# k^T v of batches 0 and 1 in full-width matmuls, and a part of expert 0's up projection around the last unit's values

## The chip, the cores and the metric

The kernel runs on one core of a Trainium2 chip (trn2). The metric is the device time of one execution in microseconds. Engines are named as in the profile: PE is TensorE's matmuls, PEld its weight loads, DVE is VectorE, ACT ScalarE, POOL GpSimd, SP SyncE, which here only issues DMAs.

## The reference

Linear attention with a decay per head (8 batches, 8 heads, 576 positions, head dimension 64), then a mixture of four experts over the 4608 x 512 result:

```python
scores = scale * q @ k^T                        # per batch and head, scale = 1/8
Dmat = where(rel >= 0, gamma[h] ** rel, 0)      # rel = position of q - position of k
x = ((scores * Dmat) @ v).transpose -> [4608, 512]
p = domain_probs / (domain_probs.sum(-1) + 1e-9)
out = sum over e of p[:, e] * (relu(x @ w1[e]) @ w2[e])     # w1: 4 x 512 x 1024, w2: 4 x 1024 x 512
```

## The kernel before

The decay is split into a factor on k and a factor on q, so that a chunk of positions needs three things: its own masked scores times v (`values_own`), its q times the sum of k^T v over all chunks before it (`values_carried`), and k^T v of its own for the chunks after it (`kv`). The 64 x 64 sums of two heads stand as diagonal blocks in a 128 x 128 tile of `sbd`, whose other blocks stay zero; so one matmul with 128 x 128 weights does a pair of heads.

Batches 0 and 1 are done in `Unit`s: four per batch, each half of 512 positions (`hf`) for four of the eight heads (`g`). Batch 0 comes first, in the order (hf, g) = (0,0), (1,0), (0,1), (1,1), called units 0 to 3 here; u is the index in the loop at L650. A unit's steps are:

- `cast` (L498): k and q times their decay to bf16 on DVE, v on POOL.
- `trans_pe` (L509): transposes of k and q on PE into `pt`, one ACT copy (L519) to `qkT`.
- `scores` (L531): 16 matmuls with 64 x 64 weights (L540), then the mask on DVE, `sT` (L542).
- `kv` (L547): matmuls into `kvp0` (L559), one per pair of rows r and half j of a head pair, with weights of 64 columns and 64 or 128 rows. The first block of a half sums 64 partitions, the second 128; in batch 0 a unit with hf = 1 also adds the whole first half. ACT copies both halves j to `sbd` (L578). In batch 1 the first half's total goes to `carry` with a DVE copy (L580), and the second half adds it while it writes `sbd` on DVE (L575).
- `values_own` (L586, L593), `values_carried` (L597, L603), then ACT copies the output to `xt` (L619), the transposed input of the experts: one call for each of two head pairs, which are two of the four 128-row parts (dc) of the up projection's contraction.

All PSUM tiles come from one ring of four buffers of two banks each (`ring_tile`). `warm(n)` (L135) issues n matmuls on zeros with 512 columns (L138).

The order on each engine is the program's order, written out by hand. After the loop of batch 0 the first tile of 512 tokens goes through the experts: `up_group` (L353) for pairs of 128-row parts of the hidden layer (i = 0 to 3; 16 matmuls of 512 columns at L359, relu on ACT at L363 for this tile), then `down_plain` (L372, L378) with its sums on DVE (L388, L390). Between these groups the steps of batch 1 and of batch 0's last 64 positions run at places given by the table `slots`: place n is run after group n. `v_head` is scores and kv of a unit of batch 1; units 2 and 3 of it have their transposes done by DMA from SP (L525). Weights are loaded on POOL's queue in a fixed order: w1 of expert 0 in two halves (`load_w1_at`), w2 of expert 0, w1 of expert 1 and so on. From the second tile on, the down projection uses seven products (L451) and the later batches use the class `Duo` with its own `kv` (L255), which the change leaves alone.

Of the kernel before, what the change touches and what calls it, by code (L numbers as in the profile page):

```python
# [11 lines left out]
Copy = mybir.ActivationFunctionType.Copy  # L12
Exp = mybir.ActivationFunctionType.Exp
Relu = mybir.ActivationFunctionType.Relu
# [9 lines left out]
def kernel(  # L24
# [10 lines left out]
    nc = tc.nc  # L35
    B, H, S, D = q.shape
# [9 lines left out]
    NDC = Dm // 128  # L46
# [19 lines left out]
    def ring_tile(name, shape, dt=FP32):  # L66
        return ring.tile(shape, dt, tag="ring", name=name)
# [25 lines left out]
    w1_sb = [const.tile([128, NDC, F], BF16, name=f"w1_{e}") for e in range(E)]  # L93
# [5 lines left out]
    def load_w1(e, f=slice(0, F)):  # L99
        return nc.gpsimd.dma_start(out=w1_sb[e][:, :, f], in_=moe_w1[e][:, f].rearrange("(dc p) f -> p dc f", p=128))  # L100
# [10 lines left out]
    NU = 4  # L111
# [23 lines left out]
    def warm(n):  # L135
        w = ring_tile("w", [128, 512])
        for _ in range(n):
            nc.tensor.matmul(w, lhsT=zz[:, 0:128], rhs=zz, start=True, stop=True)  # L138
# [69 lines left out]
    def mixing_weights():  # L208
        nc.vector.tensor_reduce(psm, prb, axis=mybir.AxisListType.X, op=ADD)
        nc.vector.tensor_scalar_add(psm, psm, 1e-9)  # L210
        nc.vector.reciprocal(psm, psm)
        nc.vector.tensor_tensor(pn, prb[:, :, :].rearrange("p t e -> p e t"),
                                psm.unsqueeze(1).to_broadcast([128, E, NTT]), op=MULT)
        nc.sync.dma_start(out=pd[:, :].rearrange("e (p t) -> p e t", p=128), in_=pn)
# [3 lines left out]
    def load_p(t, e, eng):  # L218
        pB[t, e] = ppool.tile([128, NT], FP32, tag="pB", name="pB")
        eng.dma_start(out=pB[t, e], in_=pd[e:e + 1, t * NT:(t + 1) * NT].to_broadcast([128, NT]))  # L220
# [4 lines left out]
    def xt_of(t):  # L225
        if t not in xt:
            xt[t] = xpool.tile([128, NDC, NT], BF16, tag="xt", name="xt")
        return xt[t]


    class Duo:
        def __init__(self, b, d):
            self.b, self.d = b, d
            self.ps = slice(2 * d, 2 * d + 2)
            self.qT, self.kT, self.sT = {}, {}, {}
# [14 lines left out]
        def kv(self):  # L250
            kvp = ring_tile("kvp", [128, 2, NC, D])
            for i, p in self.pairs():
                for c in range(NC):
                    for j in range(2):
                        nc.tensor.matmul(kvp[64 * j:64 * j + 64, i, c:NC, :], lhsT=bfs[p % 2]["k"][:, c, j, :],  # L255
                                         rhs=bv[p][:, c, j, :].unsqueeze(1).to_broadcast([128, NC - c, D]),
                                         start=(i == 0 and c == 0), stop=(c == NC - 1), skip_group_check=True)
            for j in range(2):
                r = slice(64 * j, 64 * j + 64)
                nc.scalar.activation(sbd[r, self.ps, :, r], kvp[r], Copy)  # L260
# [92 lines left out]
    def up_group(h, t, e, i):  # L353
        ph = ring_tile("ph", [128, 2, NT])
        x = xt_of(t)
        for f in range(2):
            fc = 2 * i + f
            for dc in range(NDC):
                nc.tensor.matmul(ph[:, f, :], lhsT=w1_sb[e][:, dc, fc * 128:(fc + 1) * 128],  # L359
                                 rhs=x[:, dc, :], start=(dc == 0), stop=(dc == NDC - 1))  # L360
        fk = e * NFC + 2 * i
        if t == 0:
            nc.scalar.activation(h[:, fk:fk + 2, :], ph, Relu)  # L363
            return
        nc.vector.scalar_tensor_tensor(h[:, fk:fk + 2, :], ph, 0.0,  # L365
                                       pB[t, e][:, :].unsqueeze(1).to_broadcast([128, 2, NT]), op0=MAX, op1=MULT)
        if i == NFC // 2 - 1 and t + 1 < n_nt:
            load_p(t + 1, e, nc.gpsimd)

    acc0 = {}  # L370

    def down_plain(h, t, e, ns):  # L372
        m, g = divmod(ns, 2)
        if g == 0:
            acc0["po"] = ring_tile("po", [128, 2, Dm])
        po = acc0["po"]
        for fc in range(NFC):
            nc.tensor.matmul(po[:, g, :], lhsT=h[:, e * NFC + fc, ns * 128:(ns + 1) * 128],  # L378
                             rhs=wx[e // 2][:, (e % 2) * NFC + fc, :, :].rearrange("p a b -> p (a b)"),
                             start=(fc == 0), stop=(fc == NFC - 1))  # L380
        if g == 0:
            return
        if e == 0:
            acc0[m] = spool.tile([128, 2, Dm], FP32, tag="S", name="acc0")
        for g in range(2):
            pe = pm0[:, 2 * m + g, e:e + 1]
            if e == 0:
                nc.vector.tensor_scalar_mul(acc0[m][:, g, :], po[:, g, :], pe)  # L388
            else:
                nc.vector.scalar_tensor_tensor(acc0[m][:, g, :], po[:, g, :], pe, acc0[m][:, g, :], op0=MULT, op1=ADD)  # L390
        if e == E - 1:
            for g in range(2):
                n0 = t * NT + (2 * m + g) * 128
                nc.sync.dma_start(out=out[n0:n0 + 128, :], in_=acc0[m][:, g, :])
# [95 lines left out]
    class Unit:  # L490
# [54 lines left out]
                tri0[:, :, :, :].rearrange("p r s t -> p (r s t)").unsqueeze(1).to_broadcast([128, 4, 2 * C]), op=MULT)  # L545

        def kv(self):  # L547
            kvp = ring_tile("kvp0", [128, 2, 2, D])
            hf = self.hf

            def mm(g, rows, dst, hh, first):
                for r in range(2):
                    for j in range(2):
                        lhsT = self.bf("k", hh)[0:rows, r, 2 * g + j, :]
                        rhs = self.bf("v", hh)[0:rows, r, 2 * g + j, :]
                        o = kvp[64 * j:64 * j + 64, g, dst, :]
                        if dst == slice(0, 2):
                            rhs = rhs.unsqueeze(1).to_broadcast([rows, 2, D])
                        nc.tensor.matmul(o, lhsT=lhsT, rhs=rhs, start=(first and r == 0), stop=False,  # L559
                                         skip_group_check=True)  # L560

            first = True
            for g in range(2):
                if hf == 1 and self.carry is None:
                    mm(g, 128, slice(0, 2), 0, first)
                    first = False
                mm(g, 64, 0, hf, first)
                first = False
                mm(g, 128, 1, hf, False)
            gs = slice(2 * self.g, 2 * self.g + 2)  # L570
            for j in range(2):
                jr = slice(64 * j, 64 * j + 64)
                dst = sbd[jr, gs, 2 * hf:2 * hf + 2, jr]
                if hf == 1 and self.carry is not None:
                    nc.vector.tensor_tensor(dst, kvp[jr],  # L575
                                            self.carry[jr, gs, :].unsqueeze(2).to_broadcast([64, 2, 2, D]), op=ADD)
                else:
                    nc.scalar.activation(dst, kvp[jr], Copy)  # L578
            if hf == 0 and self.carry is not None:
                nc.vector.tensor_copy(self.carry[:, gs, :], kvp[:, :, 1, :])  # L580

        def values(self):
            self.values_own()
# [53 lines left out]
    def cast_unit(u):  # L637
        us[u].cast("k", nc.vector)
        us[u].cast("q", nc.vector)
        us[u].cast("v", nc.gpsimd)  # L640
        if u in load_w1_at:
            load_w1(*load_w1_at[u])
# [7 lines left out]
    for u in range(NU):  # L650
        if u + 2 < NU:
            cast_unit(u + 2)
        us[u].values_own()
        if u + 1 < NU:
            us[u + 1].scores()
        us[u].values_carried()
        if u + 2 < NU:
            us[u + 2].trans_pe(1)
        if u + 1 < NU:
            us[u + 1].kv()  # L660
        if u == NU - 2:
            warm(2)
    mixing_weights()
    early.close()
    hp = ctx.enter_context(tc.tile_pool(name="hp", bufs=1))
    h = hp.tile([128, E * NFC, NT], BF16, name="h")
    first = ctx.enter_context(ExitStack())
    fpool = first.enter_context(tc.tile_pool(name="fpool", bufs=1))
    q1 = fpool.tile([128, 2, 2, 4, D], BF16, name="q1")
# [43 lines left out]
    def run(slots, i):  # L713
        for f in slots.get(i, []):
            f()
# [33 lines left out]
    n = 0  # L749
    for e in range(E):  # L750
        for i in range(4):
            up_group(h, 0, e, i)
            run(slots, n)
            n += 1
        for m in range(4):
            down_plain(h, 0, e, m)
            run(slots, n)
            n += 1
# [13 lines left out]
    for b in range(2, B):  # L772
        g = NS * (b - 3)
# [24 lines left out]
    for t in range(1, n_nt):  # L798
        d = [Down(h, t, s) for s in range(2)]
# [5 lines left out]
        n = NS * (t - 1)  # L805
# [40 lines left out]
```

## Time and profile before

| what | value |
|---|---|
| median of 4 runs | 536.35 us (535.85 to 536.38) |
| profiled execution | 536.37 us, span 534.7 us |
| PE busy | 527.5 us, 99% of the span |
| DVE, POOL, ACT busy | 361.6, 146.3, 87.2 us |
| chain that ended last | PE 95%, DVE 2%, ACT 1%, DMA 1% |
| granted TensorE clock | nine tenths or more of full speed in every slice of the page |
| DMA | 63.56 MB, 119 GB/s over the span |

Times in the views are microseconds from the start of the span. A busy PE is a PE with a matmul in flight, so its share says little by itself; the chain says what a later end hangs on. In the groups and timelines a line gives start, busy time, engine, line, operation, output<-inputs, the shape and count, and in brackets the idle time before it with what ended it.

### The profile page before, as it was taken

Reading aid. Unit: us, or ns where it says so; the run is one execution under the profiler, and the core shown is the slowest. Engines: PE = TensorE matmul, PEld = TensorE weight load, DVE = VectorE, ACT = ScalarE, POOL = GpSimd, SP = SyncE. Lnnn points to the kernel's source line nnn. Section 1 sums busy time; section 2 is a strip of 40 time slices with the busy share of each in tenths; the row PEclk is TensorE's granted clock in tenths of the full one; section 3 lists DMA queues with packets and bytes.
Section 4 is the critical chain, followed back from the end, with each engine's and each line's share of the span. In section 5 each row is a group of like instructions: output and inputs, shape, how many; then the busy total and the mean of one; then the engine's idle time right before and its main releaser. Section 6 shows DMA issues by size and latency. Waiting matters only on the chain.

```text
span 534.7 us, 10343 instructions
## 1 busy us (share of the span) xinstructions
PE 527.5 (99%) x4318; PEld 339.5 (63%) x4318; DVE 361.6 (68%) x454; ACT 87.2 (16%) x175; POOL 146.3 (27%) x188
## 2 busy tenths in 40 slices
PE   8999999999999999999999999999999999999997
PEld 4544454468745885478646865587548844884586
DVE  6425668896587767797578767777765567556754
ACT  4623450012101121020101001100110000000010
POOL 5734004245235344335132603153000000000000
PEclk9999999999999999999999999999999999999999
DMA  9999947678768766726353744454010111110001
GB/s 243 207 209 250 237 122 190 148 170 155 153 153 170 160 148 150 174 67 161 104 137 97 150 133 113 106 119 125 21 41 24 56 40 39 40 44 18 0 31 50
DMA packets 145119, 63.56 MB, mean 119 GB/s; under 512 B 124240, under 2 KB 135888, under 8 KB 145072
## 3 DMA queue, kind: packets, MB, share of 16 engines
q1 hardware_dynamic: 134752, 43.50, 34.5%
q0 software_dynamic: 10176, 19.27, 16.2%
q8 instruction: 34, 0.56, 0.4%
q10 hardware_dynamic: 144, 0.13, 0.1%
q14 instruction: 13, 0.11, 0.1%
HBM read 53.56 MB, written 9.51 MB: 118 GB/s over the span
## 4 chain that ended last, share of the span: by engine, by line
PE 95%; DVE 2%; ACT 1%; DMA 1%; issue 0%; SPq 0%; DVEq 0%
PE ph L359 47%; PE pd L451 37%; PE po L378 5%; PE kvp L255 1%; PE o L280 1%; PE s L269 1%; PE o L284 1%; ACT qkT L519 1%; DMA raw_0q<-in_q_dram 1%; DVE h L365 0%; DVE sT L542 0%; PE kvp L559 0%; PE s L540 0%; PE pt L517 0%; PE o L603 0%; PE w L138 0%
## 5 line engine op out<-in xcount | busy, mean ns | idle before, releaser
L359 PE MATMUL ph<-xt,w 128*128 128x512 bf16 x1152 | 254.7, 379 | 0.4 <-DVE h L365 0.2
L365 DVE SCALAR_TENSOR_TENSOR h<-ph,pB 128x1024 bf16<-128x1024 f32 x128 | 156.5, 1224 | 57.7 <-PE ph L359 57.7
L359 PEld LDWEIGHTS <-w 128*128 128x128 bf16 x1152 | 110.9, 98 | 129.5 <-issue 0.6
L451 PEld LDWEIGHTS <-h 128*128 128x128 bf16 x1024 | 99.8, 98 | 13.2
L451 PEld LDWEIGHTS <-s 128*128 128x128 bf16 x768 | 75.0, 98 | 8.7
L451 PE MATMUL pd<-wx,h 128*128 128x256 bf16 x512 | 61.1, 273 | 0.0
L451 PE MATMUL pd<-wx,s 128*128 128x256 bf16 x512 | 61.1, 273 | 0.0
L220 POOL DMA_DIRECT2D pB<-pd x28 | 15.7, 562 | 155.6 <-DVE h L365 142.7
L486 POOL TENSOR_TENSOR ob<-v,p 128x256 f32<-128x256 f32 x15 | 11.7, 783 | 114.3 <-DVE v L483 92.8
L239 POOL TENSOR_TENSOR bf_k<-raw_k,gk 128x512 bf16<-128x512 f32 x24 | 25.9, 1079 | 31.6 <-DMA raw_k<-in_k_dram 20.0
L260 ACT ACTIVATE sbd<-kvp 64x512 bf16<-64x512 f32 x24 | 14.2, 592 | 121.5 <-PE kvp L255 121.3
L271 DVE TENSOR_TENSOR sT<-s,tri 128x1024 bf16<-128x1024 f32 x24 | 28.3, 1219 | 7.5 <-PE s L269 7.5
L428 DVE TENSOR_TENSOR s<-s,h 128x1024 bf16<-128x1024 bf16 x32 | 30.9, 1006 | 0.0
L451 PE MATMUL pd<-t4w,h 128*128 128x256 bf16 x256 | 30.6, 273 | 0.0
L451 PE MATMUL pd<-t2w,s 128*128 128x256 bf16 x256 | 30.6, 273 | 0.0
L451 PE MATMUL pd<-t3w,h 128*128 128x256 bf16 x256 | 30.6, 273 | 0.0
L378 PE MATMUL po<-wx,h 128*128 128x512 bf16 x128 | 29.1, 379 | 0.1
L459 ACT ACTIVATE p<-pd 128x256 f32<-128x256 f32 x16 | 6.2, 384 | 138.9 <-PE pd L451 106.2
L239 POOL TENSOR_TENSOR bf_q<-raw_q,gq 128x512 bf16<-128x512 f32 x24 | 27.2, 1134 | 3.4 <-DMA raw_q<-in_q_dram 2.8
L432 DVE TENSOR_TENSOR s<-h,s 128x1024 bf16<-128x1024 bf16 x32 | 25.6, 839 | 0.0
L426 DVE TENSOR_TENSOR s<-h 128x1024 bf16<-128x1024 bf16 x32 | 23.8, 784 | 0.0
L468 DVE TENSOR_TENSOR u<-pd,p 128x256 f32<-128x256 f32 x16 | 6.8, 425 | 23.9 <-PE pd L451 23.8
(153 smaller groups left out, 364.6 us busy)
## 6 DMA issues: line engine op xcount, KB each, us to landing
pB<-pd POOLq DMA_DIRECT2D x28, 256.0 KB, 3.6
raw_k<-in_k_dram SPq DMA_DIRECT2D x48, 128.0 KB, 2.5
raw_q<-in_q_dram SPq DMA_DIRECT2D x48, 128.0 KB, 2.9
raw_v<-in_v_dram SPq DMA_DIRECT2D x48, 128.0 KB, 3.0
wx<-in_moe_w_dram POOLq DMA_DIRECT2D x4, 1024.0 KB, 15.3
out_dram<-oa SPq DMA_DIRECT2D x16, 256.0 KB, 2.2
out_dram<-ob SPq DMA_DIRECT2D x15, 256.0 KB, 2.4
w<-in_moe_w_dram POOLq DMA_DIRECT2D x3, 1024.0 KB, 15.1
```

The source lines that it names most:

```text
L220: eng.dma_start(out=pB[t, e], in_=pd[e:e + 1, t * NT:(t + 1) * NT].to_broadcast([128, NT]))
L239: eng.tensor_tensor(bfs[p % 2][n], raw1[n], g[:, :, 2 * p:2 * p + 2].unsqueeze(3).to_broadcast([128, NC, 2, D]), op=MULT)
L260: nc.scalar.activation(sbd[r, self.ps, :, r], kvp[r], Copy)
L271: nc.vector.tensor_tensor(sT[:, :, :, :].rearrange("p j c t -> p (j c) t"), s[:, :, :, :].rearrange("p j c t -> p (j c) t"), tri[:, :].uns ...
L359: nc.tensor.matmul(ph[:, f, :], lhsT=w1_sb[e][:, dc, fc * 128:(fc + 1) * 128], rhs=x[:, dc, :], start=(dc == 0), stop=(dc == NDC - 1))
L365: nc.vector.scalar_tensor_tensor(h[:, fk:fk + 2, :], ph, 0.0, pB[t, e][:, :].unsqueeze(1).to_broadcast([128, 2, NT]), op0=MAX, op1=MULT)
L378: nc.tensor.matmul(po[:, g, :], lhsT=h[:, e * NFC + fc, ns * 128:(ns + 1) * 128], rhs=wx[e // 2][:, (e % 2) * NFC + fc, :, :].rearrange("p ...
L426: nc.vector.tensor_tensor(self.alloc("s1")[:, l], h[:, l, self.b], h[:, r, self.b], op=ADD)
L428: nc.vector.tensor_tensor(self.alloc("s2")[:, l], self.s1[:, l], h[:, l, self.a], op=SUB)
L432: nc.vector.tensor_tensor(self.alloc("s4")[:, l], h[:, r, self.a], self.s2[:, l], op=SUB)
L451: mm = nc.tensor.matmul(dst, lhsT=src[:, kk, tok], rhs=rhs(c), start=(start and c == 0), stop=(c == KH - 1), skip_group_check=True)
L486: nc.gpsimd.tensor_tensor(self.ob[:, HF:Dm], self.v, self.p5, op=ADD)
```

## The change

In `kv` both heads of a pair are taken together: weights of 128 columns and a right side of 128 columns (256 where the first half is added for two blocks) give 128 x 128 products, of which only the diagonal blocks are read. `kvp0` grows to a full bank, the 128-row matmuls of both pairs g come first and the 64-row ones last. The copies to `sbd` read the diagonal blocks; the copy to `carry` is made per half j.

The first two of the four up groups of expert 0 (tile 0) are cut by tokens instead: `UpHalf(0)` is hidden parts 0 to 3 for tokens 0 to 255, `UpHalf(1)` the same for tokens 256 to 511. Eight of the 16 matmuls of `UpHalf(0)` are issued before the values of batch 0's last unit, the other eight right after them, and `UpHalf(1)` follows. `warm(2)`, which stood between unit 3's kv and its values, is gone.

```diff
+    class UpHalf:
+        def __init__(self, half):
+            self.c = slice(256 * half, 256 * half + 256)
+            self.ph = ring_tile("ph", [128, 4, 256])
+
+        def matmuls(self, i):
+            for fc in range(2 * i, 2 * i + 2):
+                for dc in range(NDC):
+                    nc.tensor.matmul(self.ph[:, fc, :], lhsT=w1_sb[0][:, dc, fc * 128:(fc + 1) * 128],
+                                     rhs=xt_of(0)[:, dc, self.c], start=(dc == 0), stop=(dc == NDC - 1))
+
+        def relu(self, h):
+            nc.scalar.activation(h[:, 0:4, self.c], self.ph, Relu)
...
         def kv(self):
-            kvp = ring_tile("kvp0", [128, 2, 2, D])
+            kvp = ring_tile("kvp0", [128, 2, 2, 128])
             hf = self.hf
-
-            def mm(g, rows, dst, hh, first):
+            first = [True]
+
+            def mm(g, rows, dst, hh):
                 for r in range(2):
-                    for j in range(2):
-                        lhsT = self.bf("k", hh)[0:rows, r, 2 * g + j, :]
-                        rhs = self.bf("v", hh)[0:rows, r, 2 * g + j, :]
-                        o = kvp[64 * j:64 * j + 64, g, dst, :]
-                        if dst == slice(0, 2):
-                            rhs = rhs.unsqueeze(1).to_broadcast([rows, 2, D])
-                        nc.tensor.matmul(o, lhsT=lhsT, rhs=rhs, start=(first and r == 0), stop=False,
-                                         skip_group_check=True)
-
-            first = True
+                    two = lambda n: self.bf(n, hh)[0:rows, r, 2 * g:2 * g + 2, :].rearrange("p j d -> p (j d)")
+                    rhs = two("v")
+                    if dst == slice(0, 2):
+                        rhs = rhs.unsqueeze(1).to_broadcast([rows, 2, 128])
+                    nc.tensor.matmul(kvp[:, g, dst, :], lhsT=two("k"), rhs=rhs, start=first[0], stop=False,
+                                     skip_group_check=True)
+                    first[0] = False
+
+            if hf == 1 and self.carry is None:
+                for g in range(2):
+                    mm(g, 128, slice(0, 2), 0)
             for g in range(2):
-                if hf == 1 and self.carry is None:
-                    mm(g, 128, slice(0, 2), 0, first)
-                    first = False
-                mm(g, 64, 0, hf, first)
-                first = False
-                mm(g, 128, 1, hf, False)
+                mm(g, 128, 1, hf)
+            for g in range(2):
+                mm(g, 64, 0, hf)
             gs = slice(2 * self.g, 2 * self.g + 2)
             for j in range(2):
                 jr = slice(64 * j, 64 * j + 64)
                 dst = sbd[jr, gs, 2 * hf:2 * hf + 2, jr]
+                src = kvp[jr, :, :, jr]
                 if hf == 1 and self.carry is not None:
-                    nc.vector.tensor_tensor(dst, kvp[jr],
+                    nc.vector.tensor_tensor(dst, src,
                                             self.carry[jr, gs, :].unsqueeze(2).to_broadcast([64, 2, 2, D]), op=ADD)
                 else:
-                    nc.scalar.activation(dst, kvp[jr], Copy)
-            if hf == 0 and self.carry is not None:
-                nc.vector.tensor_copy(self.carry[:, gs, :], kvp[:, :, 1, :])
+                    nc.scalar.activation(dst, src, Copy)
+                if hf == 0 and self.carry is not None:
+                    nc.vector.tensor_copy(self.carry[jr, gs, :], kvp[jr, :, 1, jr])
...
     for u in range(NU):
         if u + 2 < NU:
             cast_unit(u + 2)
+        if u == NU - 1:
+            part = UpHalf(0)
+            part.matmuls(0)
         us[u].values_own()
...
         if u + 1 < NU:
             us[u + 1].kv()
-        if u == NU - 2:
-            warm(2)
+    part.matmuls(1)
     mixing_weights()
     early.close()
     hp = ctx.enter_context(tc.tile_pool(name="hp", bufs=1))
     h = hp.tile([128, E * NFC, NT], BF16, name="h")
+    part.relu(h)
+    part = UpHalf(1)
+    part.matmuls(0)
+    part.matmuls(1)
+    part.relu(h)
...
     for e in range(E):
         for i in range(4):
-            up_group(h, 0, e, i)
+            if e > 0 or i > 1:
+                up_group(h, 0, e, i)
             run(slots, n)
```

## The prediction, made before the changed kernel had run

> **What bounds the kernel now.** The profiled execution took 536.37 us, its span is 534.7; the median of the four runs is 536.35. Sums are made on the span and taken off the median one for one. First the page: busy shares and chain.
>
> ```profile
> PE 527.5 (99%) x4318; PEld 339.5 (63%) x4318; DVE 361.6 (68%) x454; ACT 87.2 (16%) x175; POOL 146.3 (27%) x188
> ...
> PE 95%; DVE 2%; ACT 1%; DMA 1%; issue 0%; SPq 0%; DVEq 0%
> ```
>
> TensorE carries 95% of the chain, so only less work on PE, or less waiting by it, can count. Next the chain in order of time, where the change sits (start, length, what):
>
> ```profile
> 17.52 1.07 PE kvp L559 x24
> 18.59 0.54 PE w L138 x2
> ...
> 19.84 0.47 ACT xt L619
> ...
> 20.35 6.72 PE ph L359 x30
> ```
>
> Before 20.35 the chain passes between ACT and PE; from there PE is nearly alone. Then PE's timeline of that place (start, busy us, line, out<-in, weights, output, count, idle before):
>
> ```profile
> 16.41 0.41 PE L540 MATMUL s<-qkT 64*64 64x128 bf16 x13
> 17.05 0.25 PE L540 MATMUL s<-qkT 64*64 64x128 bf16 x3 [0.23 <-issue]
> 17.23 0.29 PE L603 MATMUL o<-qkT,sbd 128*128 128x128 bf16 x2
> 17.45 1.14 PE L559 MATMUL kvp<-bf_v,bf_k 128*64 128x128 bf16 x24
> 18.52 0.61 PE L138 MATMUL w<-zz 128*128 128x512 bf16 x2
> 19.05 0.42 PE L593 MATMUL o<-sT,bf_v 64*64 64x128 bf16 x16
> 19.40 0.40 PE L603 MATMUL o<-qkT,sbd 128*128 128x128 bf16 x4
> 19.64 1.09 PE L359 MATMUL ph<-xt,w 128*128 128x512 bf16 x3
> ```
>
> Two matmuls of zeros (L138) stand between kv and values. The first up projection starts at 19.64, does two matmuls, and stops: by single starts the third is at 20.346 and the fourth at 20.651, each 50 ns after one of the two ACT copies of xt (from 19.84) ends. The seventeenth, the first of group i=2, which the change leaves as it is, starts at 23.458. That is the point I compare.
>
> **Rates**, start to start of single matmuls in this trace: the same shape of weights in a row 56 ns for 128 columns, 109 for 256 (24.45 us for 224 at L451), 216 for 512. Where the shape of the weights changes (128x128, 128x64, 64x64), the next matmul starts about 93 ns after the stream ends: 149 after 128 columns (L593 to L603), 122 to 128 after 64, 309 after 512 (L138 to L593). In kv the two halves j start 3 ns apart, so they already run side by side.
>
> **kv of batch 0.** From the matmul before it to the one after it, kv takes 872, 1215, 870 and 1218 ns for units 0 to 3, with up to five changes of shape. The wide form for units 1 and 3: 56 (the matmul before has 128x128 weights as well), four of 256 columns 428, four of 128 columns 168 to the last, change 149, three steps of 67, 56, 56, change 149: 1129, which is 0.09 us less. Units 0 and 2: 701, 0.17 less. Of this unit 0 gives nothing, since ACT starts its sbd copy when qkT is done, and unit 2 nothing for the same reason. Unit 1 gives 0.09: its sbd copy at 13.41 waits for kvp, and ACT would be free at 13.32; all later links follow. The 64-row step with 128x128-wide output is a form that this trace lacks; between no change of shape at all and a change at every step, I take one change in and one out, as between 128x64 and 64x64 here.
>
> That the halves j run side by side (3 ns) speaks against going wide, but the changes of shape fill most of the old 1.07 us. The Trainium skill, TensorEngine Tiling (Array Packing), Theoretical Speedup, says that a stationary side of up to 64 columns, packed twice, runs up to twice as fast; by that alone, as an estimate, wide kv would double in units 1 and 3 and in batch 1, and the sum would end some 2 us slower than before.
>
> **The pause.** At 16.6 to 17.05 PE stands still within scores, and the view names no releaser ("issue"). It comes after some 448 matmuls and weight loads; the new order has 56 fewer by then and reaches that count only within values of unit 3, some 2.5 us later. I take it as gone. Then the two L603 of unit 2 wait for the sbd copy instead, which by the 0.09 above ends at 16.92: they start at 16.97 instead of 17.23, of which 0.17 is due to the pause.
>
> **Around the last values.** From there: second L603 at 17.04, kv from 17.10, its next at 18.17. Eight matmuls of 256 columns (108 each) take the place of the zeros; the last starts at 18.93, values at 19.13 (107 + 93), L603 at 19.48 to 19.65, eight more from 19.71, the half for tokens 256 to 511 from 20.57. Its third and fourth need the xt copies: ACT starts 0.256 after the last L603, at 19.91, and by the old lengths these are through at 20.42 and 20.73; PE wants them at 20.79 and 20.90. So no wait is left. Sixteen of 108 end at 22.30, where i=2 starts: 1.16 less than 23.458. The extra 16 weight loads are hidden (98 ns under 108), and two relu calls of 1024 elements replace two, in the same places of ACT's queue; no DMA moves in its queue. Covers: the first half of w1 lands at 17.15 (issue 9.35, 7.8 to landing), wanted at 18.17; the first w2 at 25.19 by its landings, wanted at 25.7 instead of 26.9; xt of unit 2 at 18.12, wanted at 18.49; and q of batch 1's first unit, landed at 49.79, is cast at 51.16, then 50.1. Past these covers each wait would give back its own length.
>
> **Batch 1.** In the middle kv follows scores, both with 64x64 weights:
>
> ```profile
> 66.92 0.77 PE L559 MATMUL kvp<-bf_v,bf_k 64*64 64x64 bf16 x16
> ...
> 68.53 0.29 DVE L580 COPY carry<-kvp 128x128 f32<-128x128 f32 x1 [0.17 <-ACT sbd L578]
> ...
> 82.51 0.17 PEld L603 LDWEIGHTS <-sbd 128*128 128x128 bf16 x3 [0.32 <-DVE sbd L575]
> ```
>
> Here the old form needs no change at its start: 748 ns. The new: 149 + 67 + 56 + 56 + 149 + 179 + 149 = 805. So 0.06 is lost in each of units 0 and 1; in units 2 and 3 it goes into PE's waits for DVE (0.19 at 81.75 and the line above). The carry copy becomes two, and the order of the new kernel shows that ACT's second sbd copy waits for DVE's first carry copy, which stands behind sT (68.4). ACT's second copy ends near 69.13 instead of 68.50, DVE's second carry copy at 69.47 instead of 68.82, and behind it the four casts of units 2 and 3 with their DMA transposes on SP, 0.7 later. q of unit 2 landed at 73.40, wanted at 75.19: hidden. The pB and raw loads behind them on SP are 0.7 later too; the first raw remainder is then cast near 87.4 and needed after 94. L603 of unit 1 wants sbd at 69.80, relu of i=1 moves by 0.15 and PE needs its buffer at 73.4.
>
> Sum: -1.16 + 0.11 = -1.05 us, so 535.3. From 20 to 84 us PE otherwise waits only for relu (0.2 four times), which moves along.
>
> **Rivals.** A, as summed, 535.0 to 535.5: chance 0.58. C, going from 128 to 64 rows at full width is no change of shape: two changes less (0.19) in unit 3 and 0.13 below the old time in each of batch 1's units 0 and 1, so -1.16 - 0.19 - 0.26 = -1.6, 534.7: 0.19. For it speaks that the output columns stay 128 wide; against it, every change of rows in kv costs 122 or more. The same page of the skill, Key Properties, says that a change of tiling mode drains TensorE, and lists 64x128 as a mode of its own; that would leave A. D, the pause comes back at its old count, which is then within values of unit 3, on a PE without slack: -1.16 + 0.50 + 0.11 = -0.55, 535.8: 0.08. B, slower: weights of 64 rows and 128 columns are never loaded ahead, so each of the three steps in a kv costs a whole change. At 149 that is 0.28 per kv: +0.26 in unit 1, +0.28 in unit 3, +0.56 in two of batch 1, +0.13 in the others beyond DVE's cover: +0.18 in all, 536.5. At 268, the longest step after a kv (79.47 to 79.74), it is 0.64 per kv and some +2.3, 538.7. It turns slower at about 140 per step. Chance 0.15.
>
> **Numbers.** 0.2%, about what a measurement of this kernel can tell from no change, is 1.07 us, 535.28, in the middle of A. A gives faster 0.34 and same 0.24; C faster 0.19; D same 0.08; B slower 0.12 and same 0.03. The range takes in C, D and the lower end of B: 534.6 to 536.5.
>
> **What would show it.** Right: no idle PE from the first kv of unit 3 to group i=2, which starts near 22.3; wide kv at 56 per step with two changes; the two carry copies 0.7 apart with scores of unit 2 unmoved behind ph. Wrong: steps of 150 between 64-row matmuls (B), none above 67 (C), a gap without releaser in values of unit 3 (D), or a wait for w1, w2 or xt where I count a cover.

## The result, and the profile after

The changed kernel takes 535.52 us (median of 38 runs, 534.85 to 537.8), the kernel before beside it 536.36 (60 runs). The ratio is 0.9984 with a 95% interval of 0.9979 to 0.9989: 0.86 us less, between 0.6 and 1.1. The interval leaves out no change, so it is faster, but by less than the 0.2% (1.07 us) that the prediction called no change. The forecast was 535.3.

Two points on counting. An up group is eight matmuls of 512 columns (L359 has 32 for the four groups of expert 0), not 16 as the description of the kernel before has it; the two groups that were cut are 16 of 512, or 32 of 256 columns. And some records of matmuls are missing from some traces, so that a count such as x15 in a view below can stand for 16.

The profiled execution of the changed kernel took 536.1 us, with a span of 534.4, against 536.37 and 534.7. So this one trace shows only 0.3 of the 0.86 us, and the question is what the other executions had that this one lacked. The page first, the busy shares and the chain:

```profile
PE 527.1 (99%) x4260; PEld 340.3 (64%) x4260; DVE 360.1 (67%) x456; ACT 87.2 (16%) x175; POOL 145.0 (27%) x188
...
PE 93%; DMA 3%; SPq 2%; DVE 1%; issue 0%; POOL 0%; DVEq 0%
```

PE's busy time hardly moved. The line to look at is the chain: DMA holds 3% instead of 1%. The chain in order of time, from 12 to 30 us (start, length, what), says which transfers these are:

```profile
9.57 5.24 DMA raw_3v<-in_v_dram
...
14.86 0.55 POOL bf_v L520
15.41 10.97 DMA wx<-in_moe_w_dram
26.38 0.14 issue
26.52 3.61 PE po L394 x16
```

In the kernel before, this stretch of the chain was PE's and ACT's. Now it is read backwards so: the first down projection (`po`, L394) starts 0.14 after w2 of expert 0 landed, at 26.38; w2 was issued at 15.41, because its issue stands on POOL's queue behind the cast of v of unit 3; and that cast waited for its own load until 14.81. So here PE waits for a load that the prediction had landed at 25.19, before it was wanted. PE's own line says the same (from the timeline of 25 to 27.5 us):

```profile
26.52 1.24 PE L394 MATMUL po<-wx,h 128*128 128x512 bf16 x5 [0.29 <-DMA wx<-in_moe_w_dram]
```

PE's timeline of the changed place (start, busy us, line, out<-in, weights, output, count, idle before):

```profile
16.57 0.42 PE L556 MATMUL s<-qkT 64*64 64x128 bf16 x16 [0.25 <-ACT qkT L535]
17.23 0.28 PE L619 MATMUL o<-qkT,sbd 128*128 128x128 bf16 x2 [0.24 <-ACT sbd L594]
17.35 1.15 PE L574 MATMUL kvp<-bf_v,bf_k 128*128 128x256 bf16 x12
18.43 1.05 PE L380 MATMUL ph<-xt,w 128*128 128x256 bf16 x8
19.41 0.42 PE L609 MATMUL o<-sT,bf_v 64*64 64x128 bf16 x16
19.76 0.40 PE L619 MATMUL o<-qkT,sbd 128*128 128x128 bf16 x4
19.99 2.78 PE L380 MATMUL ph<-xt,w 128*128 128x256 bf16 x24
22.61 0.59 PE L359 MATMUL ph<-xt,w 128*128 128x512 bf16 x2
```

From 17.35 to the group i=2 (L359 at 22.61) no line has an idle time in brackets: the zeros are gone, the 24 matmuls run through, and the wait for xt is gone with them. The scores before it run as 16 in one group, without the pause. In batch 1, from the timeline of all engines between 60 and 78 us:

```profile
66.69 0.72 PE L574 MATMUL kvp<-bf_v,bf_k 128*128 128x128 bf16 x8
...
67.95 0.27 DVE L596 COPY carry<-kvp 64x128 f32<-64x128 f32 x1
68.25 0.38 ACT L594 ACTIVATE sbd<-kvp 64x256 bf16<-64x256 f32 x1 [0.43 <-DVE carry L596]
68.67 0.29 DVE L596 COPY carry<-kvp 64x128 f32<-64x128 f32 x1 [0.45 <-ACT sbd L594]
```

The two carry copies start 0.72 apart, as the order of instructions had said; in the order of time the next thing on DVE, the casts, starts at 68.99 instead of 68.74, which is 0.58 later counted from the scores of unit 1 (66.34 here, 66.67 before), where the prediction had 0.7. No wait of PE grows by it: batch 1 loses 0.115 in all, and the two kv ahead of the casts account for that below.

To set runs side by side whose first loads came at other times, the experiments use distances between starts of single matmuls: t0 is the start of the last transpose of unit 3, i=2 the first matmul of the third up group, `po` the first matmul of the first down projection, and after it come the first transposes of batch 1, the first matmul of the second tile of tokens (tile 1), and the last matmul.

| distance, us | before | after | after, without its wait |
|---|---|---|---|
| t0 | 15.019 | 15.183 | |
| t0 to i=2 | 8.435 | 7.431 | 7.431 |
| t0 to `po` | 11.888 | 11.336 | 10.884 |
| `po` to batch 1 | 30.252 | 30.250 | |
| batch 1 to tile 1 | 27.261 | 27.375 | |
| tile 1 to the last matmul | 446.28 | 446.28 | |

The wait of 0.452 is what is left of 11.336 over 10.884, the distance (to 0.002) in all later executions of this order in which w2 was there in time. The column of after has t0 later by 0.16 because the first loads came later in this execution: t0 stands 5.31 after the start of unit 1's copy to `qkT` on ACT in all ten traces with the wide kv in batch 0, and 5.40 in the four with the old one, and that copy starts at 9.87 here, 1.21 after q of unit 1 landed, and at 9.62 before. 0.164 - 0.552 + 0.114 is -0.27, the 0.3 between the two spans.

### The profile page after: what moved, and what is told of

Its sections match the earlier page's. It is cut to its first block, busy times and chain, and to the rows that moved or that the text cites. A ratio compares the mean times of both kernels' runs of the same rounds, so it can differ in the third digit from the quotient of the medians.

```text
span 534.4 us, 10227 instructions
## 1 busy us (share of the span) xinstructions
PE 527.1 (99%) x4260; PEld 340.3 (64%) x4260; DVE 360.1 (67%) x456; ACT 87.2 (16%) x175; POOL 145.0 (27%) x188
## 4 chain that ended last, share of the span: by engine, by line
PE 93%; DMA 3%; SPq 2%; DVE 1%; issue 0%; POOL 0%; DVEq 0%
PE ph L359 45%; PE pd L467 37%; PE po L394 5%; DMA wx<-in_moe_w_dram 2%; SPq L117 2%; PE kvp L255 1%; PE o L280 1%; PE s L269 1%; PE o L284 1%; DMA raw_3v<-in_v_dram 1%; DVE h L365 0%; PE kvp L574 0%; PE s L556 0%; DVE acc L406 0%; DVE sT L558 0%; PE o L619 0%
## 5 line engine op out<-in xcount | busy, mean ns | idle before, releaser
L359 PE MATMUL ph<-xt,w 128*128 128x512 bf16 x1136 | 251.0, 379 | 0.2 <-DVE h L365 0.2
L359 PEld LDWEIGHTS <-w 128*128 128x128 bf16 x1136 | 109.4, 98 | 127.3
L467 PEld LDWEIGHTS <-h 128*128 128x128 bf16 x1024 | 99.8, 98 | 13.2
L394 PE MATMUL po<-wx,h 128*128 128x512 bf16 x128 | 29.1, 379 | 0.3 <-DMA wx<-in_moe_w_dram 0.3
L484 DVE TENSOR_TENSOR u<-pd,p 128x256 f32<-128x256 f32 x16 | 6.8, 425 | 25.7 <-PE pd L467 25.7
```

The lines of the kernel that those rows point to most:

```text
L467: mm = nc.tensor.matmul(dst, lhsT=src[:, kk, tok], rhs=rhs(c), start=(start and c == 0), stop=(c == KH - 1), skip_group_check=True)
```

## The experiments

The theory: the change brings PE forward by some 0.8 to 1.0 us, about as summed, and the one load of w2, whose margin it eats up, takes back up to 0.5 us of that in those executions in which it lands late. The rival: w2's lateness is a matter of that one execution and costs the timed runs nothing; what is missing to the forecast was lost for good in PE's own steps, in the wide kv of batch 1 above all.

**1. w2 of expert 0 as two transfers.** The down projection uses the parts of w2 in order, so a first half that lands early is enough to start it; four matmuls, 0.86 us, later it needs the second.

```diff
-    def load_w2(e):
+    def load_w2(e, lo=0, hi=NFC):
...
-    load_w2(0)
+    load_w2(0, 0, NFC // 2)
+    load_w2(0, NFC // 2, NFC)
```

> The changed kernel with w2 of expert 0 loaded by two DMAs of 512 KB instead of one of 1024 KB. Theory W (the missing part of the gain is a wait for w2: in the changed kernel's profile PE finished its up groups at 26.07 and started down at 26.52, just after the load landed at 26.38): the first half lands 2 to 3 us earlier, down starts right behind up, 1.0 to 1.2 us below before. Rival K (the missing part is in batch 1's kv): stays at 0.8 to 0.9 below.

Measured: 535.39 us (median of 9 runs) against 536.35; ratio 0.9979 (0.997 to 0.9988). The profiled execution took 535.35, its span is 533.6. The halves landed at 21.93 and 25.63. Its timeline, 21.5 to 26.5 us:

```profile
22.30 3.62 PE L359 MATMUL ph<-xt,w 128*128 128x512 bf16 x15
...
25.75 1.03 PE L394 MATMUL po<-wx,h 128*128 128x512 bf16 x4
```

L394 has no idle time before it any more, and starts 10.884 after t0. That agrees with theory W, but this trace does not show that the halves took the wait away: its second half landed at 25.63, and a start 0.14 after that would have been only 0.02 later than the 25.75 seen. The same holds for the other traces with halves below, where it would have been 0.04 at most. That the wait in the trace of after is a wait for w2 rests on the views of after, and on experiments 3 and 5, where `po` starts 0.13 and 0.14 after w2 again. By time the version is 0.96 below before, between the two expectations, and the gain over the change alone (0.9979 against 0.9984) is smaller than the intervals.

**2. The wide kv alone.** The kernel before with the new `kv`, its `warm(2)` and its whole up groups kept.

```diff
-            kvp = ring_tile("kvp0", [128, 2, 2, D])
+            kvp = ring_tile("kvp0", [128, 2, 2, 128])
...
         if u == NU - 2:
             warm(2)
```

> Only the full-width kv, in batches 0 and 1; the zeros and the up groups as before. By the prediction's terms: unit 1 0.09, the pause 0.17, unit 3's first step 0.09 less, batch 1 0.11 more: 0.24 below before, the pause in scores of unit 3 gone. Rival P (the full width gives nothing, the whole gain is the rearranged up projection): no difference, or slower by 0.1.

Measured: 536.09 us (12 runs); ratio 0.9994 (0.9986 to 1.0003), which can't be told from no change (0.24 was expected). PE's timeline around kv of unit 3 (L138 is x2 in the program; one record is missing):

```profile
16.63 0.28 PE L603 MATMUL o<-qkT,sbd 128*128 128x128 bf16 x2 [0.24 <-ACT sbd L578]
16.75 1.15 PE L558 MATMUL kvp<-bf_v,bf_k 128*128 128x256 bf16 x12
17.84 0.39 PE L138 MATMUL w<-zz 128*128 128x512 bf16 x1
```

The old kv in that place takes 1.218 us from the matmul before it to the matmul after it, the wide one here 1.139. t0 to `po` is 11.642; batch 1 to tile 1 is 27.378, 0.117 more than before. Of what unit 1 and unit 3 gain, 0.08 each, batch 1 takes most back. The pause in scores of unit 3 is gone.

**3. The up projection alone, with the old kv.** Run twice; the diff is against the changed kernel.

```diff
-            kvp = ring_tile("kvp0", [128, 2, 2, 128])
+            kvp = ring_tile("kvp0", [128, 2, 2, D])
...
         if u == NU - 1:
             part = UpHalf(0)
             part.matmuls(0)
```

> Only the up projection around the last values; kv as before. By the prediction's terms: 4.13 us from the eight first matmuls to group i=2, from 18.52: 22.65 instead of 23.46, so 0.8 below before; PE reaches down near 26.1, after w2 has landed in a run like that of before (25.2). Rival P: the same 0.85 as the whole change.

> The up projection around the last values with the old kv, again, since in the profile of its first run the v of unit 3 landed late (17.92) and kv waited for it. Without that: 11.89 - 0.76 = 11.13 us from the last transpose to down, with the pause in scores of unit 3 still there; tile 1 27.26 after batch 1's first transposes, as before. Rival P: 10.88, as the whole change.

Measured: 535.8 us (12 runs), ratio 0.9997 (0.9985 to 1.0008), and 535.62 (12 runs), ratio 0.9985 (0.9972 to 0.9998). The first profiled execution says nothing of the changed stretch: v of unit 3 landed at 17.92 there, three microseconds late, and PE waited for that. In the second, `po` waits for w2 as in the trace of after (the chain from 14 to 29 us, its last three links):

```profile
15.51 11.38 DMA wx<-in_moe_w_dram
26.89 0.14 issue
27.02 2.10 PE po L394 x9
```

The wait is 0.639. Without it t0 to `po` is 10.994, where 11.13 was expected, and the pause in scores is back, after 13 of the 16 matmuls, worth 0.03 here and not the 0.17 that the expectation had put in. Batch 1 to tile 1 is 27.263, that of before. So the 0.11 of batch 1 belong to the wide kv, and nearly all of the gain to this part.

**4. Both mended: halves of w2, and the old kv in batch 1 alone.** Run twice; `kv_narrow` is the old `kv`, called in batch 1 only.

```diff
-        vs[u].kv()
+        vs[u].kv_narrow()
...
-    load_w2(0)
+    load_w2(0, 0, NFC // 2)
+    load_w2(0, NFC // 2, NFC)
```

> The changed kernel with kv of batch 1 as before (narrow) and with w2 of expert 0 in two DMAs. Theory W with the prediction's 0.11 for batch 1: 1.1 to 1.3 below before, 0.1 better than the version with w2 in halves alone. Rival K: 1.0 below, all of the step from 0.85 due to the narrow kv.

> The changed kernel with batch 1's kv as before and w2 in halves, again, beside the next one on the same chip: 27.26 to tile 1, no wait for w2, 1.0 to 1.1 below before.

Measured: 535.56 us (11 runs), ratio 0.9982 (0.9972 to 0.9992), and 535.64 (11 runs), ratio 0.9989 (0.9979 to 0.9999). Both traces have t0 to `po` at 10.88 and batch 1 to tile 1 at 27.263. So on PE the 0.115 come back in full and stay. The device times, 0.79 and 0.69 below before, miss the 1.0 to 1.3 expected and are no better than experiment 1; the spans of the same executions do show it. Their median is 533.5 us in both sets, 1.1 below the 534.6 of the kernel before beside them, and that of experiment 1 is 533.7. In nearly all other runs the device time is 1.6 to 1.8 us longer than the span; in these two sets it is up to 3.3 longer, with medians of 1.95 and 1.85. What passes in that time outside the span no view here shows. By the same medians of the span the change alone stands at 533.8, 0.8 below 534.6.

**5. The narrow kv in batch 1, without the halves.**

```diff
-        vs[u].kv()
+        vs[u].kv_narrow()
```

> The changed kernel with batch 1's kv as before. 27.26 us from batch 1's first transposes to tile 1 instead of the 27.375 of the changed kernel, so 0.1 below the changed kernel, but with the wait for w2 left: 0.95 below before by time. Rival K: the whole of the missing 0.2 comes back.

Measured: 535.88 us (12 runs); ratio 0.9996 (0.9979 to 1.0013), too wide to say anything. Its profiled execution took 540.25, and its timeline from 16 to 23 us shows why:

```profile
19.36 0.62 POOL L520 CAST bf_v<-raw_3v 128x512 bf16<-128x512 f32 x1 [5.83 <-DMA raw_3v<-in_v_dram]
...
20.03 0.86 PE L574 MATMUL kvp<-bf_v,bf_k 128*128 128x128 bf16 x8 [2.20 <-POOL bf_v L520]
```

v of unit 3 landed at 19.31, some 4.5 us later than in the trace of after; the kv waited 2.2 us for its cast, w2's issue, which is behind that cast, came at 19.91 instead of 15.41, and `po` waited another 0.97 us for a w2 that landed at 30.65. Batch 1 to tile 1 is 27.262: that much of the expectation can be read.

**6. The changed kernel itself, twice more.** No edit.

> The changed kernel once more. From the start of the last transpose of unit 3 to the first down matmul the work without a wait is 10.88 us (11.89 before). Theory W: down starts there or 0.14 us after w2 has landed, whichever is later; w2 lands 5.2 to 5.4 us after the second half of w1. Time 0.8 to 0.9 below before. Rival K: a delay of 0.4 in every run, whatever the landing.

> The changed kernel, third look, same chip: 10.88 to down or the landing of w2 plus 0.14, whichever is later; 0.8 to 0.9 below before by time, 0.2 to 0.3 above the version with w2 in halves.

Measured: 536.28 us (12 runs, up to 540.81), ratio 1.0006 (0.9988 to 1.0025), and 535.55 (12 runs), ratio 0.9988 (0.9974 to 1.0001). The profiled executions took 535.73 and 535.05. The chain of the first, from 14 to 28 us, its last two links:

```profile
23.13 3.19 PE ph L359 x14
26.31 1.73 PE po L394 x8
```

Here the chain stays on PE through the down projection: w2 landed at 25.97, 0.18 before `po` started, and t0 to `po` is 10.884. In the second it landed at 25.09 with the same distance. So the wait is not a part of the change that every execution pays: 0.45 in one trace, nothing in two. The times say less than was expected of them: the first set shows no gain (0.2 us by the medians, where 0.8 to 0.9 was expected, with five of its 12 executions above 537), and the second, 0.78 below before, lies 0.09 below experiment 4's second set and not 0.2 to 0.3 above the version with halves; by the median of the span it is 0.3 above it (533.8 and 533.5).

**7. A test of the pause: the zeros at the start of the kernel before, 16 short ones for 8 long ones.** Eight matmuls more before the same place; one execution.

```diff
-    warm(8)
+    w8 = ring_tile("w", [128, 512])
+    for i in range(16):
+        nc.tensor.matmul(w8[:, 0:256], lhsT=zz[:, 0:128], rhs=zz[:, 0:256], start=True, stop=True)
```

> The kernel before, with the eight first matmuls on zeros (512 columns) made sixteen of 256 columns: the same stream, 16 more PE instructions. Theory I (the pause hangs on the count of instructions): in scores of unit 3 it comes 16 matmuls and weight loads earlier, after about 5 of its 16 matmuls instead of 13. Theory T (it hangs on time or on what the other engines do): after about 13 as before.

Measured: 536.59 us in one run. PE's timeline at scores of unit 3 and behind them:

```profile
16.80 0.42 PE L540 MATMUL s<-qkT 64*64 64x128 bf16 x16
17.46 0.28 PE L603 MATMUL o<-qkT,sbd 128*128 128x128 bf16 x2 [0.24 <-ACT sbd L578]
```

There is no pause at all, neither where it was nor earlier, and t0 to `po` is 11.719 instead of 11.888. So in this one execution the count of matmuls alone does not set it. Two things go with it in all traces: PE pauses after 13 of the 16 scores in the traces of old-kv kernels that show a pause (before, and both of experiment 3), and each time the pause ends 2.31 to 2.46 us after the first transfer of 16 KB on one of the instruction queues has begun (14.74, 15.10 and 14.98 us). In this experiment that transfer began at 13.22. With the wide kv it begins between 13.2 and 14.7, and PE gets to the same count after 18.4 us. That PE waits there for its next instructions would fit all of it; no run takes this apart from other causes, so it is argued and not shown.

**8. The halves of w2 in reverse order.** The down projection then needs what lands last first, while the two transfers stay two. The diff is against experiment 1.

```diff
-    load_w2(0, 0, NFC // 2)
-    load_w2(0, NFC // 2, NFC)
+    load_w2(0, NFC // 2, NFC)
+    load_w2(0, 0, NFC // 2)
```

> The changed kernel with w2 of expert 0 in two DMAs, the second half first. As many DMAs as in the version with the halves in order, but what down wants first lands when the whole w2 did, 5.2 to 5.6 us after the second half of w1. Theory W: without a wait 10.88 us from the last transpose to down; the wait comes back wherever the landing plus 0.14 is later than that, 0 to 0.5 in a run with ordinary loads. Rival N (the two DMAs themselves took the wait away): 10.88 whatever the landing.

Measured: 535.57 us (10 runs); ratio 0.9989 (0.9979 to 0.9998). Inconclusive: in its profiled execution all of w2 had landed at 25.19, before PE wanted it at 25.51, so that the order of the halves could make no difference there. Whether the two transfers as such, or their order, keep the wait away stays open.

**9. A version that goes further: halves of w2, and in batch 1 the 64-row matmuls of kv first.** Scores before it have 64-row weights, the up projection after it 128 x 128; so the 128-row ones last leave one change of shape fewer at the end. The diff is against experiment 1.

```diff
-            for g in range(2):
-                mm(g, 128, 1, hf)
-            for g in range(2):
-                mm(g, 64, 0, hf)
+            parts = ((128, 1), (64, 0))
+            for rows, dst in parts if self.carry is None else parts[::-1]:
+                for g in range(2):
+                    mm(g, rows, dst, hf)
```

> The changed kernel with w2 in halves in order, and in batch 1 the 64-row matmuls of kv ahead of the 128-row ones, so that the kv ends in the shape of what follows it. One change of shape less per kv: 149 + 67 + 56 + 56 + 149 + 67 + 56 + 56 + 56 = 0.71 us instead of 0.80, so 27.19 from batch 1's first transposes to tile 1 (27.375 in the changed kernel, 27.26 before). If the shape is not what counts: 27.375. By time 1.0 to 1.2 below before.

Measured: 534.99 us (11 runs) against 536.33; ratio 0.998 (0.9972 to 0.9989), the fastest median of all versions and ahead of both kernels. The profiled execution took 534.86, its span is 533.2. PE's timeline in batch 1:

```profile
65.21 0.42 PE L556 MATMUL s<-qkT 64*64 64x128 bf16 x16
65.56 0.72 PE L574 MATMUL kvp<-bf_v,bf_k 64*128 64x128 bf16 x8
66.12 1.89 PE L359 MATMUL ph<-xt,w 128*128 128x512 bf16 x8
```

From the last of scores to the first of ph: the changed kernel has 805 (change 149, steps 66, 56, 56, change 152, steps 66, 56, 56, change 148), this one 709 (148, 67, 56, 55, 149, 66, 56, 56, and 56 into ph), the kernel before 748. Batch 1 to tile 1 is 27.165: 0.21 less than in the changed kernel, 0.10 less than before. The medians put it 0.4 us ahead of experiment 1 (533.3 against 533.7 by the span), but the intervals of the two overlap almost wholly; the 0.21 is what the traces show.

## Why the prediction was right, and where not

**The sum.** Without any wait for w2, the parts by distances of matmul starts are:

| part | predicted | measured | from |
|---|---|---|---|
| up around the last values | -0.81 | -0.75 | 11.719 (experiment 7, old order without pause) to 10.965 (experiment 3, without wait and pause) |
| kv of unit 3 | -0.09 | -0.08 | 11.719 to 11.642 (experiment 2) |
| sbd copy of unit 1 | -0.09 | -0.08 | start of unit 2's qkT copy to t0: 2.62 in all four traces with the old kv in batch 0, 2.54 to 2.53 in the ten with the wide one |
| the pause | -0.17 | 0 to -0.17 | 11.719 against 11.888 |
| batch 1 | +0.11 | +0.115 | 27.261 to 27.377 (experiment 2 and others) |
| sum | -1.05 | -0.80 to -0.97 | |

The 0.81 is what the prediction's 1.16 leaves when its three other terms are taken off. On top of the last row comes the wait for w2: nothing in two of three executions of the changed kernel, 0.45 in one, 0.64 in the up projection alone. With 0 to 0.45 the sum stands between -0.35 and -0.97, and the timed -0.86 (-1.13 to -0.59) lies in its upper part. So rival A held as the mechanism, in its place and in its sign; by time the median is 0.02 above the 535.0 to 535.5 that A was given, and well inside the whole range. The chances leaned too far: faster had 0.53 in all and no change 0.35, and the gain stayed under the 0.2% that was to tell them apart. The terms on PE's own work came out within 0.06 each. The total is short by these, by the pause and by the wait for w2, and the timed runs don't say how much of it each of the last two makes up.

**Shape of the 64-row matmuls: right, and it sets B and C aside.** By single starts wide kv of unit 3 runs at 109 for 256 columns, 56 for 128, then 152 into the 64 rows, 67, 55, 56, and 149 out of them: 1.139 us where 1.129 was counted, and 805 in batch 1 where 805 was counted. No 64-row step after the first costs a change, which B needed at 140 or more; and going to 64 rows costs a full one, which C needed to be none. The Trainium skill, TensorEngine Tiling (Array Packing), Theoretical Speedup, was cited against the change with up to twice the speed for two packed 64-column weights; measured, the wide form is 0.08 us shorter in unit 3 (1.218 to 1.139) and 8% longer in batch 1. What the same page says under Key Properties, that a change of tiling mode drains TensorE, and its list of 64x128 among the tiling modes (under Available Configurations, not under Key Properties), agree with the steps of 152 and 149 into and out of the 64-row matmuls.

**The rival of the experiments falls in its second half.** Batch 1 loses 0.115, as counted, in every kernel with the kv of the change, and nothing in those without; everything from `po` to batch 1 and from tile 1 to the last matmul repeats within 0.01 us in most of them (experiment 8's last stretch was longer by 0.08). There is no other place in which PE lost time for good. Of its first half, that w2 is late in that one execution alone is answered by experiment 3, where `po` waits for it too; what the lateness costs the timed runs stays open, as no timed comparison here is fine enough to show it.

**The cover of w2: the step that failed.** The prediction counted 0.5 us of cover, 25.19 against a need at 25.7. The need was right to 0.1, counted from t0: 25.7 is 10.77 after the t0 of 14.93 that the prediction's 0.09 leaves of 15.02, and 10.88 was measured (26.07 in the trace of after, 26.15 and 25.45 in the two other executions of the changed kernel). The landing was one execution's. In the seven profiled executions with w2 in one transfer and v of unit 3 on time it was 25.09, 25.19, 25.48, 25.97, 26.38, 26.74 and 26.89, a spread of more than three times the cover. Part of it is the start, which moves t0 as well; counted from t0 the landings are 10.17 to 11.50, and four of the seven are later than the 10.74 up to which `po` would not wait in the new order. In the old order `po` came at 26.9 in the trace of before and 27.1 in that of experiment 7, each time with w2 there, so that the scatter did not show. The chain of after shows where part of the spread comes from: the issue stands behind v's cast, and v landed at 14.07 before and 14.81 after, so 0.74 of the 1.19 are there before w2 is even issued. The prediction had its own warning, that past a cover each wait gives back its own length; it lacked the spread of the landing. By its own list of signs, a wait for w2 where it counts a cover is one of being wrong.

**The pause: the term that was mis-sized.** It was taken off in full, 0.17. It is gone in the traces of every kernel with the wide kv in batch 0, also in values of unit 3, so rival D falls. With the old kv it was worth 0.17 in the one trace of before, 0.03 in the second of experiment 3 and nothing in experiment 7, whose order is that of before with eight matmuls more; so the count from which the prediction argued is not enough to set it, and how often the kernel before has it in its timed runs is not known. That it went away is what the prediction said; that this is due to the count is not shown. The remaining 0.06 of the first row is mostly the rate: the steps of 256 columns took 109 and not 108, and the first one behind kv 119, which is 0.05 over the 32.

**The hidden parts were hidden.** The two carry copies are 0.72 apart and DVE's casts start 0.58 later, counted from the scores; the longer kv of units 2 and 3 in batch 1 shows nowhere, for 0.115 is twice the 0.057 of units 0 and 1. xt of the last unit and the first half of w1 ended no wait.

## What to carry to other kernels

Price a matmul by the distance from start to start, and count each change of weight shape as an item of its own: the same eight wide matmuls took 724 ns for 870 in unit 2, between transposes and values, and 805 for 748 in batch 1, between scores and an up group. Putting like shapes next to each other turned that loss around (748 before, 805 with the change, 709 with the 64-row matmuls first). A move that brings an engine forward uses up the margin of every load behind it, and that margin has to be taken from several executions and from the chain of issues ahead of the load, not from the one trace at hand. Splitting the load so that the part wanted first lands first should give margin back: the first halves landed 2.7 to 3.8 us before the down projection began in the three kernels that had them in order, and the second halves are wanted 0.86 us into it. That it saved time is not shown, since in these traces the whole of w2 had landed before the down projection began.

## What the runs showed of the hardware that was not expected

The same load at the start of the same program lands at quite different times: v of unit 3 between 14.07 and 14.90 us in twelve traces, at 17.92 and 19.31 in two whose times were 538 and 540 us, in kernels whose early loads are the same. What follows the first down projection repeats to 0.01 us in all traces up to batch 1 (30.25), so the scatter between the traced executions is made before it. The loads account for it where it can be followed: in nine of the fourteen traces unit 1's copy to `qkT`, on which t0 hangs, starts 1.20 to 1.21 after q of unit 1 has landed (at 8.07 to 8.81).

A start after a wait for a transfer came 0.13 to 0.14 us after the landing in all three cases (26.38 to 26.52, 26.89 to 27.02, 30.65 to 30.79).
